# Closing rows in two column groups and two stores with two-dimensional patterns, in a decode layer on one core

## Chip, core, metric

One core of a Trainium2 chip. The metric is the device time of one execution in microseconds (us).

In the profile PE is TensorE, PEld its weight loads, DVE VectorE, ACT ScalarE, POOL GpSimd and SP SyncE; a q marks an engine's sequencer, which issues DMAs. A landing is the semaphore update that tells that data has arrived. The granted clock is the share of TensorE's full clock that its throttle let through.

## The reference

One decode step for 4 sequences: a layer norm modulated by a small matrix product, attention of 32 heads over the last 1024 keys and values of a cache, a second modulated norm and a feed-forward layer of 1792 units. Cut to what the argument needs:

```python
mod = (silu(c) @ w_mod).reshape(4, 6, 1, -1)          # sa, ca, ga, sb, cb, gb
x = x + ga * attention(layernorm(x) * (1 + ca) + sa)  # keys, values: 8 MB each; wq, wo: 4 MB each
h = layernorm(x) * (1 + cb) + sb
x = x + gb * (relu(h @ w1) @ w2)                      # w1 512x1792, w2 1792x512
```

The output is 4 rows of 512 bf16 values, 4 KB; the inputs are 32 MB.

## The kernel before

Everything is loaded once, in one queue issued by SP, in the order of use; w2 comes last, in five pieces of 4, 4, 3, 2 and 1 blocks of 128 rows. The last product has only 4 rows, so its 512 columns are cut into four pieces of 128 which run side by side in the four 32-column groups of TensorE. The rows of one piece lie on partitions 0, 8, 16 and 24 of the group's 32 (`BS = 8`):

```python
BS = CG // B                                  # CG = 32, B = 4
cx_sb = work.tile([2 * B, D], bf16, name="cx_sb")
nc.scalar.dma_start(out=cx_sb[0:B, :], in_=c)
nc.scalar.dma_start(out=cx_sb[B:2 * B, :], in_=A_x.rearrange("b o d -> (b o) d"))
...                                           # loads on nc.sync; constants by GpSimd
W2_CHUNKS = [(0, 4), (4, 4), (8, 3), (11, 2), (13, 1)]
...
def ffn2(m0, m1):
    for m in range(m0, m1):
        for nh in range(NH):                  # NH = 4 column groups
            nc.tensor.matmul(out=z_ps[nh * CG:(nh + 1) * CG, :], lhsT=uT32[:, m, :],
                             rhs=w2_sb[:, m, nh * DH2:(nh + 1) * DH2],
                             start=(m == 0), stop=(m == FT - 1), tile_position=(0, nh * CG))
...
nc.vector.tensor_tensor(out=zg[:], in0=z_ps[:], in1=gb2[:], op=ALU.mult)
nc.vector.tensor_tensor(out=res[:], in0=zg[:], in1=x12_ps[:], op=ALU.add)
nc.scalar.dma_start(out=out.rearrange("b o (g n) -> (o g) b n", g=NH), in_=res[::BS, :])
```

## Time and profile before

| | before |
|---|---|
| time, median of the runs beside the changed kernel | 85.73 us (85.61 to 85.98) |
| span of the profiled run (its time: 85.97 us) | 84.2 us |
| HBM read | 31.99 MB, mean 380 GB/s |
| last landing of w2 in the profiled run | 80.62 us |
| from there to the end (the tail) | 3.57 us |

The span is shorter than the time, which also holds the start and end of an execution. The tail is what can be changed without touching the loads; the prediction shows its lines.

### The profile page before, as it was taken

Reading aid. Unit: us, or ns where it says so; the run is one execution under the profiler, and the core shown is the slowest. Engines: PE = TensorE matmul, PEld = TensorE weight load, DVE = VectorE, ACT = ScalarE, POOL = GpSimd, SP = SyncE. Lnnn points to the kernel's source line nnn. Section 1 sums busy time; section 2 is a strip of 40 time slices with the busy share of each in tenths; the row PEclk is TensorE's granted clock in tenths of the full one; section 3 lists DMA queues with packets and bytes.
Section 4 is the critical chain, followed back from the end, with each engine's and each line's share of the span. In section 5 each row is a group of like instructions: output and inputs, shape, how many; then the busy total and the mean of one; then the engine's idle time right before and its main releaser. Section 6 shows DMA issues by size and latency. Waiting matters only on the chain.

```text
span 84.2 us, 2368 instructions
## 1 busy us (share of the span) xinstructions
PE 56.2 (67%) x1064; PEld 47.2 (56%) x1064; DVE 25.7 (31%) x73; ACT 23.6 (28%) x37; POOL 5.2 (6%) x20
## 2 busy tenths in 40 slices
PE   0001006999972889999999941999727579598730
PEld 0000006996772883997777801999727239588610
DVE  0104000348133100164665476950001320251320
ACT  2301001664302000487788718640100010001000
POOL 6980000000000000000000000000000000000000
PEclk9999999999996555599999999559755555555555
DMA  2799999999989999999999999999999999999500
GB/s 31 301 457 455 386 432 471 459 483 420 389 370 405 424 424 424 401 428 424 409 420 420 420 420 416 416 424 428 409 416 424 416 415 432 418 387 399 186 1 2
DMA packets 4221, 32.14 MB, mean 382 GB/s; under 512 B 492, under 2 KB 628, under 8 KB 1268
## 3 DMA queue, kind: packets, MB, share of 16 engines
q1 hardware_dynamic: 4176, 31.98, 91.7%
q8 instruction: 8, 0.13, 0.6%
q10 hardware_dynamic: 36, 0.01, 0.1%
q14 instruction: 1, 0.01, 0.0%
HBM read 31.99 MB, written 0.00 MB: 380 GB/s over the span
## 4 chain that ended last, share of the span: by engine, by line
DMA 93%; SPq 2%; PE 1%; DVE 1%; issue 0%
DMA v<-in_A_v_cache_dram 33%; DMA wo_sb<-in_A_wo_dram 24%; DMA w<-in_B_w_dram 19%; DMA k<-in_A_k_cache_dram 16%; PE z_ps L472 1%; SPq L81 1%; SPq L91 0%; SPq L90 0%; DVE zg L482 0%; DVE res L484 0%
## 5 line engine op out<-in xcount | busy, mean ns | idle before, releaser
L204 PE MATMUL ktp<-ident_k,k 128*128 128x128 bf16 x256 | 19.1, 247 | 6.5 <-DMA k<-in_A_k_cache_dram 6.5
L204 PEld LDWEIGHTS <-k 128*128 128x128 bf16 x256 | 18.1, 113 | 9.1 <-DMA k<-in_A_k_cache_dram 6.6
L209 ACT COPY kT<-ktp 128x1024 bf16<-128x1024 bf16 x16 | 15.6, 1015 | 19.0 <-PE ktp L204 18.0
L207 DVE COPY kT<-ktp 128x1024 bf16<-128x1024 bf16 x16 | 11.1, 692 | 18.0 <-PE ktp L204 17.7
L342 PE MATMUL oT_ps<-pT,v 128*128 128x16 bf16 x256 | 7.1, 172 | 2.0 <-issue 2.0
L342 PEld LDWEIGHTS <-v 128*128 128x128 bf16 x256 | 7.0, 100 | 2.1 <-issue 2.0
L216 PE MATMUL sc_ps<-kT,qpad 128*32 128x512 bf16 x64 | 5.6, 445 | 0.4 <-DVE qpad L308 0.4
L359 PE MATMUL pT_ps<-ident_bf,p_rep 128*128 128x128 bf16 x32 | 3.2, 282 | 2.9 <-DVE p_rep L353 2.9
L179 PE MATMUL tp<-ident_bf,cx_sb 8*128 8x8 bf16 x4 | 0.3, 169 | 6.6 <-DMA cx_sb<-in_A_x_dram 6.6
L359 PEld LDWEIGHTS <-p_rep 128*128 128x128 bf16 x32 | 2.8, 131 | 3.4 <-DVE p_rep L353 3.4
L304 PE MATMUL qT_ps<-hT,wq_sb 128*128 128x4 bf16 x128 | 3.5, 166 | 1.4 <-DVE ab L297 1.4
L304 PEld LDWEIGHTS <-wq_sb 128*128 128x128 bf16 x128 | 3.5, 104 | 1.5 <-issue 1.5
L179 PEld LDWEIGHTS <-cx_sb 8*128 8x128 bf16 x4 | 0.2, 112 | 6.6 <-issue 6.6
L411 ACT COPY y<-y_ps 128x256 f32<-128x256 f32 x1 | 0.4, 372 | 9.3 <-DVE y L410 9.3
L353 DVE TENSOR_TENSOR p_rep<-e_sb,mi 128x512 int32<-128x512 int32 x4 | 2.5, 687 | 0.7 <-ACT e_sb L348 0.7
L472 PE MATMUL z_ps<-w,uT 128*32 128x128 bf16 x56 | 2.2, 303 | 0.7 <-DMA w<-in_B_w_dram 0.5
L384 DVE TENSOR_TENSOR oT_sb<-oT_ps,rb 128x128 bf16<-128x128 f32 x1 | 0.3, 291 | 7.8 <-PE oT_ps L342 7.8
L418 PEld LDWEIGHTS <-wo_sb 128*128 128x128 bf16 x64 | 2.5, 120 | 0.4 <-DMA wo_sb<-in_A_wo_dram 0.4
L418 PE MATMUL y_ps<-o,wo_sb 128*128 128x4 bf16 x64 | 2.4, 173 | 0.3 <-DMA wo_sb<-in_A_wo_dram 0.3
L414 PEld LDWEIGHTS y_ps<-sel_b,y 128*128 128x128 f32 x8 | 1.8, 327 | 1.4 <-DVE y L410 1.4
L406 PE MATMUL y_ps<-wo_sb,o 128*32 128x512 bf16 x16 | 1.9, 628 | 0.9 <-DVE o L397 0.9
L216 PEld LDWEIGHTS <-qpad 128*32 128x32 bf16 x64 | 1.3, 103 | 2.2 <-DVE qpad L308 0.7
(107 smaller groups left out, 51.9 us busy)
## 6 DMA issues: line engine op xcount, KB each, us to landing
k<-in_A_k_cache_dram SPq DMA_DIRECT2D x8, 1024.0 KB, 28.1
v<-in_A_v_cache_dram SPq DMA_DIRECT2D x8, 1024.0 KB, 20.1
wq_sb<-in_A_wq_dram SPq DMA_DIRECT2D x1, 4096.0 KB, 22.5
wo_sb<-in_A_wo_dram SPq DMA_DIRECT2D x4, 1024.0 KB, 20.4
wmod_sb<-in_w_mod_dram SPq DMA_DIRECT2D x1, 2304.0 KB, 9.7
w<-in_B_w_dram SPq DMA_DIRECT2D x1, 1792.0 KB, 21.9
w<-in_B_w_dram SPq DMA_DIRECT2D x2, 512.0 KB, 19.5
wmod_sb<-in_w_mod_dram SPq DMA_DIRECT2D x1, 768.0 KB, 4.6
```

The costliest lines, as they stand in the source:

```text
L204: nc.tensor.transpose(out=tp[:, ii, :], in_=k_tiles[gi][:, iq * IQ + ii, :], identity=ident_k)
L207: nc.vector.tensor_copy(out=dst, in_=tp[:])
L209: nc.scalar.copy(out=dst, in_=tp[:])
L216: nc.tensor.matmul(out=sc_ps[hw * CG:(hw + 1) * CG, half * HALF:(half + 1) * HALF], lhsT=qpad[:, b, par, hw, :], rhs=kT[:, half * (NI // 2 ...
L304: nc.tensor.matmul(out=qT_v[:, hq, :], lhsT=wq_sb[:, t, hq * Dh:(hq + 1) * Dh], rhs=hT[:, t, :], start=(t == 0 and hq == 0), stop=(t == DT ...
L342: nc.tensor.matmul(out=oT_ps[:, hw, par].rearrange("p b r -> p (b r)"), lhsT=v_tiles[h][:, i, :], rhs=pT[:, i, c0:c0 + B * rep], start=(fi ...
L353: nc.vector.tensor_tensor(out=p_w[:, ws, :], in0=e_w[:, ws].unsqueeze(2).to_broadcast([P, WQ // 2, B]), in1=mi4[:].unsqueeze(1).to_broadca ...
L359: nc.tensor.transpose(out=tp[:, ii, :], in_=p_rep[:, i // 2, :, i % 2], identity=ident_bf[:])
L406: nc.tensor.matmul(out=y4_ps[q0:q0 + CG, :], lhsT=o4[:, l, g % 2, g // 2, :], rhs=wo_sb[:, g, l, :], start=(g == 0 and l < 4), stop=(g == ...
L414: nc.tensor.matmul(out=y_ps[:, t, :], lhsT=y4[:, t, :], rhs=sel_b[:], start=(t == 0), stop=False)
L418: nc.tensor.matmul(out=y_ps[:, m, :], lhsT=wo_sb[:, g, l, m::DT], rhs=o4[:, l, g % 2, g // 2, 0:B], start=False, stop=(g == NP - 1 and l = ...
L472: nc.tensor.matmul(out=z_ps[nh * CG:(nh + 1) * CG, :], lhsT=uT32[:, m, :], rhs=w2_sb[:, m, nh * DH2:(nh + 1) * DH2], start=(m == 0), stop= ...
```

## The change

The intent is a cheaper store. Two column groups carry the 512 columns, each in two turns: turn 0 leaves its rows on even partitions, turn 1 adds its rows on odd ones, because the weights of turn 1 are the same columns read one element earlier. So each group ends with 8 consecutive rows, stored with a two-dimensional pattern, one group by SP, the other by ACT. The two groups left free take blocks 0 to 3 of w2, which are added in ahead of time. x moves to GpSimd's queue. Cut to its core:

```diff
-    BS = CG // B
+    NX = 2
+    CP = CG + NX
-    nc.scalar.dma_start(out=cx_sb[B:2 * B, :], in_=A_x.rearrange("b o d -> (b o) d"))
+    nc.gpsimd.dma_start(out=cx_sb[B:2 * B, :], in_=A_x.rearrange("b o d -> (b o) d"))
 ...
+    def put(tile3):
+        return tile3[:, :, NX:NX + NX * B:NX]
+    def rows(tile3, j, x):
+        return tile3[:, j, NX - x:NX - x + CG]
+    def closing(parts):
+        for x in range(NX):
+            for (ps, q, j, src, rhs, start, stop, cols) in parts:
+                for g in range(2):
+                    q0 = (q + g) * CG
+                    nc.tensor.matmul(out=ps[q0:q0 + CG, cols], lhsT=rows(src, j, x), rhs=rhs(2 * x + g),
+                                     start=start and x == 0, stop=stop and x == NX - 1, tile_position=(0, q0))
 ...    # gb and x12 go through closing() too; siluT32, uT32 and xs2 are CP = 34 columns wide
+    for m in range(ZA):                       # ZA = 4: blocks 0-3 in groups 2 and 3
+        closing([zpart(m), zpart(ZA + m)])
+    nc.scalar.copy(out=zc[:], in_=za_ps[2 * CG:P, :])
+    nc.vector.tensor_tensor(out=zc[:], in0=zc[:], in1=gb2[:], op=ALU.mult)
+    nc.vector.tensor_tensor(out=zc[:], in0=zc[:], in1=x12_ps[:], op=ALU.add)
+    for m in range(2 * ZA, FT):
+        closing([zpart(m)])
 ...
-    nc.vector.tensor_tensor(out=res[:], in0=zg[:], in1=x12_ps[:], op=ALU.add)
-    nc.scalar.dma_start(out=out.rearrange("b o (g n) -> (o g) b n", g=NH), in_=res[::BS, :])
+    nc.vector.tensor_tensor(out=res[:], in0=zg[:], in1=zc[:], op=ALU.add)
+    out_v = out.rearrange("b o (x g n) -> (b o x) g n", x=NX, g=2)
+    nc.sync.dma_start(out=out_v[:, 0, :], in_=res[0:NX * B, :])
+    nc.scalar.dma_start(out=out_v[:, 1, :], in_=res[CG:CG + NX * B, :])
```

## The prediction

> **What bounds the kernel now.** I read the page's DMA row first, then the chain that ended last, then the last microseconds in the timeline, then single rows for the instructions that the change touches.
>
> The chain in order of time:
> ```profile
> 0.73 0.37 SPq L90
> ...
> 15.81 28.16 DMA v<-in_A_v_cache_dram
> ...
> 43.99 20.36 DMA wo_sb<-in_A_wo_dram
> ...
> 64.37 15.92 DMA w<-in_B_w_dram
> 80.28 0.04 issue
> 80.33 0.66 PE z_ps L472 x11
> 80.99 0.02 issue
> 81.01 0.30 DVE zg L482
> 81.31 0.02 issue
> 81.34 0.29 DVE res L484
> ```
> Nearly the whole chain is one stream of loads. The page's DMA row shows 9 tenths in nearly every slice up to the end of that stream, so the loads are never short of requests. 31.99 MB at 380 GB/s are 84.2 us: no load is removed, so about 80.3 of the 84.2 us cannot be touched by this change. What it can touch is the tail, from the landing of the last pieces of w2 to the end.
>
> The tail in the timeline (start, duration, engine, line, operation):
> ```profile
> 78.25 1.10 PE L472 MATMUL z_ps<-w,uT 128*32 128x128 bf16 x32 [0.21 <-DVE uT L467]
> ...
> 79.66 0.51 PE L472 MATMUL z_ps<-w,uT 128*32 128x128 bf16 x12 [0.31 <-DMA w<-in_B_w_dram]
> ...
> 80.33 0.64 PE L472 MATMUL z_ps<-w,uT 128*32 128x128 bf16 x12 [0.15 <-DMA w<-in_B_w_dram]
> ...
> 81.01 0.29 DVE L482 TENSOR_TENSOR zg<-z_ps,gb 128x128 f32<-128x128 f32 x1 [2.28 <-PE z_ps L472]
> 81.34 0.29 DVE L484 TENSOR_TENSOR res<-zg,x_ps 128x128 bf16<-128x128 f32 x1
> 81.66 0.60 ACTq L485 DMA_DIRECT2D out_dram<-res  x1
> ```
> The reader is to see that the closing matmuls run in bursts, each released by a landing, and that nothing lies beside the last steps. The store is issued at 81.66. In the single records its first packet moves at 82.91, 1.25 us after the issue began; the packets take 0.11 us; the last of its four landings comes at 83.36. From there to 84.19 there are only the closing semaphores and barriers, 0.8 us that the change leaves alone.
>
> Rows of DMA issues (duration min/median/max in ns), which show what a pattern of more dimensions costs its sequencer:
> ```profile
> L485 ACTq DMA_DIRECT2D out_dram<-res x1: 602/602/602, 81.7 to 81.7; - x1
> ```
> ```profile
> L103 SPq DMA_DIRECT2D v<-in_A_v_cache_dram x8: 535/535/535, 15.8 to 41.6; - x8
> ```
> ```profile
> L127 SPq DMA_DIRECT2D w<-in_B_w_dram x5: 327/328/328, 56.7 to 66.8; - x5
> ```
> ```profile
> L71 ACTq DMA_DIRECT2D cx_sb<-in_c_dram x1: 568/568/568, 0.7 to 0.7; - x1
> ```
> ```profile
> L72 ACTq DMA_DIRECT2D cx_sb<-in_A_x_dram x1: 265/265/265, 1.3 to 1.3; - x1
> ```
> The k, v loads and the store have three-dimensional patterns: 535 and 602 ns. The w2 loads have two: 328. Four rows on ACT took 265, but 568 when SP was issuing at the same moment.
>
> **What the Trainium skill says.** Perfetto Trace Analysis, section "DMA Instruction — HWDGE", says that a DMA issue's span in the profile runs over the wait for a lock, the use of a descriptor generator that two sequencers share, and the push of excess semaphore counts. The 568 ns beside the 265 agree with a shared generator; one case does not prove it. DMA: Bandwidth & Descriptors, "Why a DMA increments its semaphore by 16 and not by 1", says that the number of engines is the largest up to 16 that divides the slowest dimension of both sides, and that the issuing sequencer adds the rest of 16. The old store (4x4x128 against 16 rows) should use 4: the trace has one early update and four landings, which agrees. The new stores, 8x128 each, should use 8. TensorE: Matmul & The Clock Gate, "Back-to-back issue gap", gives N / 1.2 ns between matmuls at the cold clock, 107 ns for N = 128. The records of the closing matmuls start in fours, a few ns apart within a four and 106 ns from four to four, with a granted clock of 0.50 from 76 us on: it agrees.
>
> **The change, part by part.**
>
> *x by GpSimd's queue.* ACT loses one issue of 0.27 us, GpSimd gains one before its first memset. x is needed by the first transposes, which now wait until 6.6 us; TensorE then has nothing until the first k tile at 13.36. So x may land up to 6 us later at no cost. GpSimd's set-up ends at 6.0 us and its first product with a close user, the identity for the k transposes, stands at 1.84 against 13.36. A microsecond or several more there is hidden. The order of SP's loads is the same in the changed kernel, and from the sixth k load on each waits for the same earlier load. Effect: 0.
>
> *gb and x12 in two column groups.* The matmul count is unchanged, 16 each, but gb now has two per column group and t. Its 4 fours of 106 ns become 8 pairs of 106: about +0.4 us of TensorE near 21 us. That delays the modulation, q and scores by 0.4. Loads have about 20 us between issue and landing, so the stream does not notice; and later TensorE waits for wo and again 0.43 us for w1, which absorbs it. x12 ends at 75.74 and w1 lands at 76.12. Effect: 0.
>
> *The closing matmuls.* Blocks 0 to 7 run as four pairs, still four column groups at once: 8 fours, as before. But block 4 now stands beside block 0, so the pair waits for the second w2 chunk, whose last landing is 78.69. From 78.73, 8 fours of 106 ns end before 79.62, where the third chunk lands: hidden. Blocks 8 to 13 have only two groups. Blocks 8 to 10: 6 pairs, 79.66 to 80.30, just in time for the fourth chunk (80.28). Blocks 11 and 12: 4 pairs. The first ends at 80.59 (as the first four does now), then 80.70, 80.80, 80.91. Block 13's chunk lands at 80.62, but TensorE is still streaming; its two pairs end at 81.02 and 81.12. Now they end at 80.96. Effect: **+0.16 us** on the path.
>
> *The added work.* One ACT copy (0.25, as the copy of gb) and two DVE operations (0.29 each) on the upper half: from about 79.9 to 80.8, before zg starts at about 81.17. Hidden. zg and res keep 128 columns; half the partitions save nothing[...]. res reads SBUF instead of PSUM: the scaling of the identity from SBUF, also 128 columns, took 285 ns against 287, so 0. No wait is lengthened by them.
>
> *The stores.* Two issues, one each on SP and ACT, of 8 rows with two dimensions. From issue start to first packet the three-dimensional store took 1.25 us; c's load on ACT, two-dimensional and beside SP's issue, took 0.95 (0.74 to 1.69). So **-0.30 us**, even with the other sequencer in the way. One data descriptor per engine instead of four: the packets take perhaps 0.03 instead of 0.11, **-0.07**. The wait for the write's landing, 0.34, stays.
>
> Sum: +0.16 - 0.30 - 0.07 = -0.21 us. 85.74 - 0.2 = about **85.55 us**.
>
> **The rivals.** First, *the two issues block each other*: both wait for the same DVE operation and start within nanoseconds. If one generator serves them in turn and the second takes 0.57 or more, as c did, plus a cold start on ACT after 80 us without an issue, the store path gains only the 0.07 and the matmuls cost 0.16: 85.85. For it speaks 568 against 265; against it that c's first packet came soon all the same and that its partner had 128 rows, not 8.
>
> Second, *TensorE becomes the bound of the tail*. Counted from the second chunk's landing at 78.69, the changed kernel has 20 steps of 106 ns, 2.1 us, ending within a few hundredths of the load-bound count. Odd weight offsets (the second column set starts one 2-byte element off) or late fours could cost 10 to 30 ns a step; with 12 steps after the third chunk that would be +0.1 to +0.35, so 85.65 to 85.9. Against it: weight loads of 32 columns lie under the running matmul in the present trace.
>
> Third, *the issue gain is all there and nothing else is lost*: if SP and ACT do not meet and each issue takes 0.27 to 0.33 us, the landing may come 0.4 earlier, and with the other terms as above 85.4. Fourth, *the software queue costs something outside the chain*, a delayed start of the stream or a longer end on GpSimd: nothing in the trace of before can show it, since no load uses that queue; I allow +0.3.
>
> **Range and chances.** The three parts on the path are a few tenths each, with opposite signs. The rivals span 85.4 to 85.9, and the three runs of before spread over 0.16, with the profiled run at 85.97; other chips add as much. So 85.1 to 86.0 for 8 in 10. Two per cent is 1.7 us; to gain that, more than half of the 3.6 us after the last landing would have to vanish, and to lose it, a new wait of 1.7 us would have to appear. Chances: faster 0.01, within 2% 0.975, slower 0.015.
>
> **What would show each step right or wrong.** In the changed profile: the stream of w still ends at about 80.3 to 80.6; the last closing matmul ends about 0.5 us after the last landing instead of 0.34; zg and res at 0.29 each; two issues of 0.27 to 0.35 (a pair of one short and one near 0.57 would speak for the first rival); first store packet about 0.95 us after res; the end about 0.2 us earlier than 84.2. The copy and the two DVE operations on the upper half must end before the last matmul. TensorE's wait for x should be below 13 us; the DMA row should stay at 9 tenths. The prediction is wrong if the first weight load or the k transposes wait for GpSimd, if zg waits for the upper half, or if the stores land later after res than the present 1.73 us.

## The result, and the profile after

85.62 us (85.49 to 85.68, 6 runs) against 85.73 (85.61 to 85.98). Ratios here are the mean time of one kernel's runs over that of the other's of the same rounds, so not quite the ratio of the medians quoted: 0.9982, 95% interval 0.9966 to 0.9999, that is 0.15 us less. That is the same by the mark of 2%, and a gain that the interval only just tells from none; the time lies inside the predicted range.

The tail of the changed kernel in the timeline:

```profile
79.48 0.26 ACT L497 COPY zc<-za_ps 64x128 f32<-64x128 f32 x1 [3.56 <-PE za_ps L194]
79.78 0.28 DVE L498 TENSOR_TENSOR zc<-zc,gb 64x128 f32<-64x128 f32 x1 [1.32 <-ACT zc L497]
80.10 0.28 DVE L499 TENSOR_TENSOR zc<-zc,x_ps 64x128 f32<-64x128 f32 x1
80.93 0.28 DVE L504 TENSOR_TENSOR zg<-z_ps,gb 64x128 f32<-64x128 f32 x1 [0.55 <-PE z_ps L194]
81.25 0.28 DVE L506 TENSOR_TENSOR res<-zg,zc 64x128 bf16<-64x128 f32 x1
81.56 0.37 SPq L508 DMA_DIRECT2D out_dram<-res  x1
81.56 0.31 ACTq L509 DMA_DIRECT2D out_dram<-res  x1
```

The added copy and its two operations end at 80.38, and zg still waits 0.55 us for TensorE (the bracket): they are hidden. The stores are issued in 0.37 and 0.31 us instead of 0.60, though at the same moment.

Because two profiled runs end their streams at different moments whatever the kernel, the tails are best laid side by side from the last landing of w2. From the single records of both traces, in us:

| step | before | after | difference | predicted |
|---|---|---|---|---|
| last landing of w2 to end of the last matmul | 0.342 | 0.544 | +0.202 | +0.16 |
| from there to the result | 0.660 | 0.637 | -0.023 | 0 |
| result to last landing of the output | 1.732 | 1.419 | -0.313 | -0.37 |
| from there to the end of the span | 0.834 | 0.908 | +0.074 | 0 |
| sum (rounded) | 3.568 | 3.508 | -0.06 | -0.21 |

The third row is itself a sum: 0.03 from the result to the issue, from the start of the issue to the first packet 1.249 before and 0.787 after (-0.46), from the first packet's start to the last one's 0.10 and 0.09, and from there to the last landing 0.35 and 0.51 (+0.16). (The prediction counted to the end of the last packet, hence its 0.11 and 0.34.)

The chain that ended last looks quite different in this profile (page, part 4):

```profile
DMA 61%; PE 30%; DVE 3%; issue 1%; SPq 1%; ACT 1%; DVEq 0%
```

It was 93% DMA. The reader should not take this for a new bound. The chain followed another branch at a v load, which waited for TensorE to free a k buffer, at most 0.5 us (SP's own waits):

```profile
SPq L105 <- PE ktp L225: 1.2, 3, 0.5
```

That load was put behind some 20 us of queued loads, and the DMA row stays at 9 tenths.

### The profile page after: what moved, and what is told of

Its sections match the earlier page's. It is cut to its first block, busy times and chain, and to the rows that moved or that the text cites. A ratio compares the mean times of both kernels' runs of the same rounds, so it can differ in the third digit from the quotient of the medians.

```text
span 83.9 us, 2373 instructions
## 1 busy us (share of the span) xinstructions
PE 56.3 (67%) x1064; PEld 47.6 (57%) x1064; DVE 26.3 (31%) x76; ACT 23.9 (28%) x38; POOL 5.9 (7%) x21
## 4 chain that ended last, share of the span: by engine, by line
DMA 61%; PE 30%; DVE 3%; issue 1%; SPq 1%; ACT 1%; DVEq 0%
DMA v<-in_A_v_cache_dram 24%; DMA w<-in_B_w_dram 23%; PE ktp L225 14%; DMA k<-in_A_k_cache_dram 14%; PE qT_ps L322 4%; PE sc_ps L237 3%; PE z_ps L194 3%; PE mT L273 2%; PE mT L275 1%; PE m_ps L259 1%; PE m_ps L262 1%; PE st_ps_var L289 1%; PE gb_ps L194 1%; SPq L93 0%; SPq L92 0%
## 5 line engine op out<-in xcount | busy, mean ns | idle before, releaser
L194 PEld LDWEIGHTS <-uT 128*32 128x32 bf16 x56 | 2.2, 136 | 0.8 <-DMA w<-in_B_w_dram 0.4
```

What stands on the lines that cost most here:

```text
L194: nc.tensor.matmul(out=ps[q0:q0 + CG, cols], lhsT=rows(src, j, x), rhs=rhs(2 * x + g), start=start and x == 0, stop=stop and x == NX - 1, ...
```

## The experiments

My theory at this point: the closing matmuls cost 0.20 us because each step takes 106 ns, the store pattern saves 0.3 us, the rest is neutral. Rivals: x's queue is what helped; two sequencers are what helped; landings set the tail and the groups don't matter.

### x alone, and all but x

`e1_x_on_act` puts x back on ACT in the changed kernel; `e2_x_alone` moves x and nothing else in the kernel before.

```diff
-    nc.gpsimd.dma_start(out=cx_sb[B:2 * B, :], in_=A_x.rearrange("b o d -> (b o) d"))
+    nc.scalar.dma_start(out=cx_sb[B:2 * B, :], in_=A_x.rearrange("b o d -> (b o) d"))
```

> The changed kernel with x put back on ACT's queue. My theory (x's queue is off the path): the load stream ends where it does in the changed kernel within the scatter of runs (last landing of w2 at 80.3 to 80.7 us), the tail from that landing to the end stays 3.5 us but for the closing barriers, which shrink from 0.91 to about 0.83 us because GpSimd's part of them is shorter without a software queue; time equal to or up to 0.1 us below the changed kernel's, ratio to before 0.996 to 0.999. Rival (moving x is what starts or ends the stream earlier and is the larger part of the 0.15 us gained): the stream ends about 0.2 us later than in the changed kernel and the ratio goes back to 1.000.

> The kernel before with x on GpSimd's queue and nothing else. My theory: closing barriers 0.08 us longer, nothing else; ratio 1.000 to 1.002. Rival (x's queue brings the gain): the last landing of w2 comes about 0.2 us earlier and the ratio is 0.997 to 0.998.

Measured: ratios 0.9976 (0.9956 to 0.9997) and 1.001 (0.999 to 1.003); the last landings of w2 at 80.33 and 80.37 us. The gain stays without the move and doesn't come with it: the rival falls. (In the changed kernel x landed at 7.25 us instead of 6.48 and the first transposes started at 7.29 instead of 6.62, well ahead of 13.2, where k is first used.)

The end of the span is less simple than I expected. GpSimd's last drain, semaphore clearing and drain take 0.078 + 0.096 + 0.034 us in the kernels without a load on its queue (5 other such kernels: at most 0.004 more) and 0.102 + 0.139 + 0.040 with one (7 other such kernels: 0.275 to 0.281 in sum): 0.07 us, as the changed kernel's last row shows. Yet e1's end was not shorter but longer, 0.997 us. Its trace shows why: SP checks the load semaphores in a fixed order, some 60 ns for each check, and without x on the other queue the stores take another pair of the eight: one store's semaphore stood fourth from the last check, so three checks were still to be made after its landing. For the same reason e2's end, 0.961, was 0.13 longer than before and not the 0.08 expected: one more check came after its store's. The move of x thus costs 0.07 us at one place of the end and spares 0.16 at another. Both are below what the timed runs resolve.

### The store's pattern

`e3_four_2d` cuts the one store of the kernel before into four two-dimensional ones, still from partitions 8 apart:

```diff
+    out_v = out.rearrange("b o (g n) -> (b o) g n", g=NH)
+    for g in range(NH):
+        eng = nc.sync if g % 2 == 0 else nc.scalar
+        eng.dma_start(out=out_v[:, g, :], in_=res[g * CG:(g + 1) * CG:BS, :])
```

> The kernel before (closing rows in four column groups) with its one store of three dimensions split into four stores of two dimensions, 4 rows each, two on SP and two on ACT. My theory (the number of dimensions sets the issue and the delay to the first packet): each issue takes 0.27 to 0.37 us, the first packet moves about 0.8 us after the first issue begins as in the changed kernel, the second pair about 0.35 us later, so the last landing comes about 1.65 to 1.75 us after the result is ready, against 1.73 before and 1.42 in the changed kernel; ratio 0.998 to 1.001. Rival A (splitting over two sequencers is what helps, whatever the dimensions): the landing comes by 1.5 us or sooner, and with the matmul tail of before the time beats the changed kernel, ratio 0.996. Rival B (landings of stores on the same engines queue behind each other, about 0.18 us each): the four groups of landings are 0.15 to 0.2 us apart.

Measured: 87.29 us, ratio 1.0171 (1.0146 to 1.0196). My theory and rival A were both missed: each issue is slow although the pattern has two dimensions, and there are two in a row on each sequencer.

```profile
L488 SPq DMA_DIRECT2D out_dram<-res x2: 638/692/747, 81.4 to 82.2; - x2
L488 ACTq DMA_DIRECT2D out_dram<-res x2: 602/651/700, 81.4 to 82.1; - x2
```

The last landing came 2.80 us after the result. Rival B fits the first two stores only, whose packets moved together and whose landings are 0.18 apart; the next two, 0.46 and 0.37 later, follow their own later packets. So I formed another theory: the step between the partitions, not the number of dimensions, makes it slow. Three runs tell them apart. `e9_stride2` is the changed kernel with its rows on every second partition (`CP` and `ident_m` follow):

```diff
-        return tile3[:, :, NX:NX + NX * B:NX]
+        return tile3[:, :, 2 * NX:2 * NX + 2 * NX * B:2 * NX]
-        return tile3[:, j, NX - x:NX - x + CG]
+        return tile3[:, j, 2 * (NX - x):2 * (NX - x) + CG]
-    nc.sync.dma_start(out=out_v[:, 0, :], in_=res[0:NX * B, :])
+    nc.sync.dma_start(out=out_v[:, 0, :], in_=res[0:2 * NX * B:2, :])      # ACT's likewise
```

> The changed kernel with the closing rows on every second partition of their column group instead of on consecutive ones; both stores still have 8 rows and two dimensions, the result is right. Theory formed after the four-store run (it is the step between partitions in SBUF, not the number of dimensions, that makes the issue and the first packet slow): issues of 0.6 to 0.75 us, first packet 1.25 to 1.35 us after the issue begins instead of 0.79, the end 0.5 us later, ratio 1.003 to 1.006. Rival (dimensions or the number of rows decide, as the prediction had it): issues of 0.30 to 0.37 us, first packet at 0.8, ratio 0.998.

```profile
L508 SPq DMA_DIRECT2D out_dram<-res x1: 793/793/793, 81.9 to 81.9; - x1
L509 ACTq DMA_DIRECT2D out_dram<-res x1: 721/721/721, 81.9 to 81.9; - x1
```

First packet 1.37 us after the issue begins: a step between partitions is enough to make a two-dimensional store slow. The ratio was 1.0105 (1.0083 to 1.0126), more than expected; its loads were slower as well, of which below. `e11_3d_unit_wrong` takes the three-dimensional pattern of before, from consecutive partitions. Its output is wrong, which doesn't matter for the time.

```diff
-    nc.sync.dma_start(out=out_v[:, 0, :], in_=res[0:NX * B, :])
-    nc.scalar.dma_start(out=out_v[:, 1, :], in_=res[CG:CG + NX * B, :])
+    nc.scalar.dma_start(out=out.rearrange("b o (g n) -> (o g) b n", g=NH), in_=res[0:NH * B, :])
```

> The changed kernel with one store on ACT in exactly the three-dimensional pattern of the kernel before (4x4x128 to HBM, 16 source rows), but from 16 consecutive partitions; the rows do not hold the whole result, so it is wrong on purpose. Step theory: issue 0.30 to 0.40 us, first packet about 0.8 us after it begins. Dimension theory (the prediction's): issue 0.55 to 0.6 us, first packet at 1.2 to 1.25. The time of the first is 0.2 to 0.3 below that of the second; ratio 0.998 against 1.001.

```profile
L508 ACTq DMA_DIRECT2D out_dram<-res x1: 702/702/702, 81.6 to 81.6; - x1
```

First packet at 1.35 us, ratio 1.004 (1.002 to 1.006): three dimensions are enough as well. So neither theory alone is right: a short issue needs both, two dimensions and consecutive partitions. The two costs don't add (before had both, 602 ns). What e11 leaves open is whether the third dimension costs, or the four rows to each landing that come with it: its 16 rows have four landings, those of `e4_one_2d_wrong` below sixteen. Four landings alone don't make a store slow, as `e10_four_unit` shows. Why this issue takes 702 ns where that of before takes 602 stays open.

`e10_four_unit` gives the kernel before consecutive rows, 4 in each group, and four stores:

```diff
-    nc.vector.tensor_scalar_max(out=uT32[:, m0:m1, ::BS], in0=us[:], scalar1=0.0)
+    nc.vector.tensor_scalar_max(out=uT32[:, m0:m1, 0:B], in0=us[:], scalar1=0.0)   # siluT32, xs2 likewise
-    nc.scalar.dma_start(out=out.rearrange("b o (g n) -> (o g) b n", g=NH), in_=res[::BS, :])
+    for g in range(NH):                                        # out_v = (b o) g n
+        eng = nc.sync if g % 2 == 0 else nc.scalar
+        eng.dma_start(out=out_v[:, g, :], in_=res[g * CG:g * CG + B, :])
```

> The kernel before with its four result rows of each column group on consecutive partitions (0 to 3 of 32) and four stores of 4 rows, two on SP and two on ACT; the result is right. Step theory: issues of 0.27 to 0.37 us, first packet about 0.8 us after the first issue begins, the second pair 0.3 to 0.4 later, last landing 1.5 to 1.75 us after the result; with the last matmul 0.34 us after the last landing of w2 the tail is within 0.15 of the changed kernel's; ratio 0.996 to 1.000. Rival (a store of 4 rows on 4 engines is slow whatever its step, as the four-store run would also allow): issues of 0.6 to 0.75 and a ratio of 1.015 or more, as in that run.

```profile
L490 SPq DMA_DIRECT2D out_dram<-res x2: 273/310/348, 80.8 to 81.2; - x2
L490 ACTq DMA_DIRECT2D out_dram<-res x2: 279/294/308, 80.8 to 81.1; - x2
```

Four rows are as quick as eight. But the landings of the four stores, four each, end at 81.95, 82.13, 82.31 and 82.49 us, 0.18 apart, although their packets moved in two close pairs. (The trace doesn't tell which engines carried them.) The same 0.18 parts the two stores of the changed kernel (82.76 and 82.95): this is the +0.16 of its third row. The ratio was 0.992 (0.9903 to 0.9937), below all expectation, and not by its tail: at 3.90 us it missed the expected 0.15 around the changed kernel's, with the landing 1.75 after the result and five more checks of SP after the store's own (an end of 1.14). Its last landing of w2 came at 79.74.

`e4_one_2d_wrong` prices a single store, 16 consecutive rows. Its output is wrong, which doesn't matter for the time.

```diff
-    nc.sync.dma_start(out=out_v[:, 0, :], in_=res[0:NX * B, :])
-    nc.scalar.dma_start(out=out_v[:, 1, :], in_=res[CG:CG + NX * B, :])
+    nc.scalar.dma_start(out=out.rearrange("b o (g n) -> (b o g) n", g=NH), in_=res[0:2 * NX * B, :])
```

> The changed kernel with one store of 16 rows and two dimensions on ACT in place of the two of 8 rows; it stores rows that do not hold the result for the second half, so it is wrong on purpose: it is the price of a single store. Theory that the second store's landing waits for the first's (in the changed kernel ACT's eight landings end at 82.76 and SP's at 82.95 though their packets move at the same time): one store lands 1.2 to 1.25 us after the result is ready instead of 1.42, and the ratio is 0.996. Rival (the late landing is a matter of the addresses or of SP's own longer issue): the landing stays at 1.35 to 1.45 us and the ratio at 0.998.

```profile
L508 ACTq DMA_DIRECT2D out_dram<-res x1: 339/339/339, 81.8 to 81.8; - x1
```

The last landing came 1.38 us after the result instead of 1.42; ratio 0.9991 (0.9965 to 1.0018). So the expected 1.2 to 1.25 was missed, and the number is the rival's. The parts say why: there is no second landing to wait for, and the landing comes 0.38 after the packets instead of 0.51, but with 16 rows the first packet comes at 0.83 instead of 0.79 and the packets take 0.14 instead of 0.09. A single store would not have been worth more closing steps. And as one sequencer does as well as two, two sequencers are not what helped.

### The closing matmuls

`e6_no_upper` runs all 14 blocks in the two lower groups:

```diff
-    for m in range(ZA):
-        closing([zpart(m), zpart(ZA + m)])
-    nc.scalar.copy(out=zc[:], in_=za_ps[2 * CG:P, :])          # and the two operations on zc
-    for m in range(2 * ZA, FT):
+    for m in range(FT):
         closing([zpart(m)])                                    # zpart: always z_ps, groups 0 and 1
```

> The changed kernel with all 14 blocks of w2 in the two lower column groups, so without the upper pair of groups, the copy and the two operations on it. Step theory (the closing matmuls are a count of steps of 106 ns at the halved clock): 28 steps follow the first without a wait that matters, so the last matmul ends about 27 x 0.106 + 0.31 = 3.2 us after the first begins, and 0.75 to 0.85 us after the last landing of w2 instead of 0.54; the tail is 0.2 to 0.3 us longer than the changed kernel's, ratio 1.000 to 1.002. Rival (landings set the tail, the groups do not matter): the distance stays at 0.55 us and the ratio at 0.998.

The last matmul ended 0.59 us after the last landing, not 0.75 to 0.85, and 2.93 us after the first began, not 3.2. The single records give the reason: 23 of the 27 steps between start times are 106 or 107 ns, the first is 79, and the last three are 64, 56 and 55. The windows show what happened then (columns: stretch, its length, busy time of the five engines, granted clock, DMA share, GB/s):

```profile
79.00:80.00 1.00, 1.00 (x24) 1.00 (x22) 0.00 (x0) 0.00 (x0) 0.00 (x0) 0.50 0.29 107
80.40:80.90 0.50, 0.47 (x14) 0.30 (x10) 0.00 (x0) 0.00 (x0) 0.00 (x0) 0.92 0.00 0
```

At 80.48, after 2.5 us of matmuls without a pause, the granted clock rose from 0.50 to 1.00, and the rest ran at nearly twice the pace. So the count of steps was right and the clock I multiplied by was not constant. Without the rise the end would have come about 0.24 us later (an estimate: the last three steps 42 to 51 ns shorter, the last matmul 0.22 instead of 0.31 us), at the expected 0.83. The rise seems to belong to the profiled run alone: it took 85.62 us at a mean clock of 0.796, the other five 85.72 to 86.03 at 0.756 to 0.777. What raised the clock no run isolates. The ratio, 1.0003 (0.9983 to 1.0023), lies at the lower end of what the step theory expected; its interval overlaps the changed kernel's 0.9966 to 0.9999, so the worth of the upper groups isn't settled beyond "small".

`e7_warm` adds matmuls nobody reads, to keep the clock up:

```diff
+    def warm(n):
+        for _ in range(n):
+            nc.tensor.matmul(out=sc_ps[:, 0:512], lhsT=ident_bf[:], rhs=pT[:, 0:4, :], start=True, stop=True)
+    ...                       # calls of 9, 3, 5, 3, 3, 3, 4, 4 and 1 in the gaps from value tile v6 on
```

> The changed kernel with some 30 matmuls of 512 columns added, whose result nobody reads, in the gaps where TensorE waits from 60 us on, to keep its clock from being halved. Theory (the closing matmuls cost the tail 0.20 us because each step takes 106 ns at the halved clock): if the granted clock is 0.9 or more from 78 us on, the steps come 55 to 65 ns apart and the last matmul ends 0.30 to 0.37 us after the last landing of w2 instead of 0.54; ratio to before 0.995 to 0.997. If the clock stays at 0.5, nothing changes but for delays of up to 0.2 us. Rival (the 0.20 us is weight loading at an odd offset or the issue of matmuls): with the clock raised the distance stays near 0.5 us.

86.64 us, ratio 1.0111 (1.0078 to 1.0144), against 0.995 to 0.997 expected: I had placed too many. (The profiled run is the slowest of the six, 87.39 us.) The nine of the first call started late and ran at half clock:

```profile
63.25 3.62 PE L396 MATMUL sc_ps<-pT,ident_bf 128*128 128x512 bf16 x8 [0.23 <-issue]
```

All later work was pushed past the loads: the last matmul ended 2.09 us after the last landing in that run. The clock did stay at 1.00 from 70 us on, and the closing steps then came 55 to 56 ns apart, so the size of a step is the clock's doing and not that of the odd weight offset. But whether a warm clock shortens the tail was not tested, since nothing in that tail waited for a landing.

### Where the loads land in SBUF

e10's stream was the puzzle. One thing differs in it that was not meant to: a new constant, `ident_m`, makes the constants ahead of the load buffers 64 bytes a partition larger, which puts every load buffer at a multiple of 512 bytes. In the kernel before they stand at 448 modulo 512, in the changed kernel at 128, in e9 at 224 (addresses as the build of each kernel assigns them). `e12_before_aligned` adds nothing but 64 unused bytes to the kernel before:

```diff
+    pad = const.tile([P, 16], f32, name="pad")     # e13: [P, 32] in the changed kernel
+    nc.gpsimd.memset(pad[:], 0.0)
```

> The kernel before with 64 bytes a partition of unused memory ahead of the load buffers, so that every load's destination starts at a multiple of 512 bytes instead of 448 modulo 512. Address theory (the four-unit run's stream ended 0.6 to 0.9 us early because its buffers happened to stand at multiples of 512): 4 MB take 9.5 us instead of 9.6 in the middle of the stream, the last landing of w2 comes at 79.6 to 79.9 us instead of 80.3 to 80.6, ratio 0.991 to 0.994. Rival (something else in that kernel, such as its stores or its contiguous rows, made the stream faster): ratio 0.998 to 1.002.

> The changed kernel with 128 bytes a partition of unused memory, so that the loads' destinations stand at 256 modulo 512 instead of 128. If a multiple of 256 is enough: the stream ends at 79.6 to 79.9 us and the ratio is 0.989 to 0.992. If it takes a multiple of 512: as the changed kernel, 0.997 to 0.999.

84.83 us, ratio 0.9876 (0.9856 to 0.9896), and for e13 84.70 us, ratio 0.9868 (0.9848 to 0.9887). Both are more than the theory expected. Last landings of w2 at 79.22 and 79.33; tails 3.57 and 3.51, as without the padding. The windows of 40 to 70 us, where only v, wo and w1 are loaded, show it best (last column GB/s): before, after, e12 and e13 in turn.

```profile
40.00:70.00 30.00, 23.24 (x496) 18.96 (x493) 12.60 (x23) 11.82 (x20) 0.00 (x0) 0.77 1.01 418
```
```profile
40.00:70.00 30.00, 23.25 (x490) 18.98 (x488) 12.18 (x23) 11.40 (x20) 0.00 (x0) 0.76 1.01 419
```
```profile
40.00:70.00 30.00, 23.59 (x502) 19.20 (x499) 12.00 (x23) 11.22 (x19) 0.00 (x0) 0.76 1.01 424
```
```profile
40.00:70.00 30.00, 23.64 (x502) 19.28 (x500) 12.04 (x23) 11.24 (x19) 0.00 (x0) 0.76 1.01 425
```

e9 has 417, e10 425. Over all runs, starts at 0 modulo 256 give 424 to 425 GB/s (four kernels), starts at 128, 192 and 224 give 417 to 420 (ten). The single records show it packet by packet: in this window a packet of 8 KB took on average 310.6 to 310.7 ns in the kernels at 0, 314.4 to 315.0 at 128, 315.5 at 192 and 316.5 at 224. (That is 4 to 6 ns a packet; the 14 KB packets of w1 save about as much, 539 against 542 to 544 ns, those of 18 and 32 KB nothing that stands out.) A multiple of 256 is enough. The Trainium skill (DMA: Bandwidth & Descriptors, "How a descriptor splits into AXI transactions") says that reads of less than a full transaction must start at a 256-byte boundary and that a descriptor starting elsewhere fetches unused bytes; here it is the destination that was moved, and the measured cost is 1.1 to 1.2% of the time (0.9876 against 1, and 0.9868 against 0.9982). This padding, of no part of the change, brings six to seven times what the change brings. e13 has the lowest median of the correct kernels; e12's interval overlaps its own.

`e14_best` was meant to add two more small things to it (its padding is 384 bytes, for a multiple of 512):

```diff
-    nc.gpsimd.dma_start(out=cx_sb[B:2 * B, :], ...)
+    nc.scalar.dma_start(out=cx_sb[B:2 * B, :], ...)
-    W2_CHUNKS = [(0, 4), (4, 4), (8, 3), (11, 2), (13, 1)]
+    W2_CHUNKS = [(0, 8), (8, 3), (11, 2), (13, 1)]
```

> The version that the runs point to: the changed kernel with load buffers at multiples of 512 bytes, x back on ACT's queue (no software queue, closing barriers 0.07 us shorter) and the first two pieces of w2 as one load, which makes the two stores take the last two of the eight load semaphores, checked last at the end. Expected: stream end 79.6 to 79.9 us, last matmul 0.55 us and result 1.18 us after it, last landing 1.42 after the result, end 0.83 after that: ratio 0.989 to 0.991. If the address theory falls: ratio 0.996 to 0.998.

85.02 us, ratio 0.9916 (0.9895 to 0.9936): slower than e13. The end did shrink to 0.834 us, but the last matmul ended 0.91 us after the last landing. The layout of w2 sets the order of w1's columns, so with a piece of 8 blocks the first layer reads the weights of blocks 0 to 7 with a step of 8 elements instead of 4 (weight loads of that layer in the changed kernel, then in e14: count, then busy us and mean ns):

```profile
L479 PEld LDWEIGHTS <-w 128*128 128x128 bf16 x56 | 1.8, 112 | 0.8 <-DMA w<-in_B_w_dram 0.8
```
```profile
L481 PEld LDWEIGHTS <-w 128*128 128x128 bf16 x56 | 2.7, 141 | 0.8 <-DMA w<-in_B_w_dram 0.8
```

These means mix all 14 blocks. In the single records the 32 loads of blocks 0 to 7 took 168 ns each and started 60 ns apart, against 118 and 33 in the changed kernel, and the means of the other 24 differ by 2 ns or less. That is 0.9 us more on TensorE just before the closing matmuls.

## Why the prediction was right

- **The stream is the bound and isn't touched.** Right as to the bound, and the reason why nothing of the change could matter much; that the buffers' addresses moved with the constants was overlooked (see the total). The last landing came at 80.35 us after and 80.62 before; e2 and e3, whose loads are those of the kernel before, ended at 80.37 and 80.35, so the 0.27 us between the two profiles is scatter of runs in the main (the profiled run of before was a long one, 85.97 us).
- **x and gb, no effect.** Right: the k transposes began at 13.22 us instead of 13.36 and x12 ended at 75.23, before w1 landed at 75.88. One named sign of being wrong came close: the page puts the wait of the first transposes, at 7.29, down to GpSimd's last memset, which ended at 7.26, just as x landed. It cost nothing.
- **Closing matmuls, +0.16.** Measured +0.20, the mechanism as told. The steps are 106 to 108 ns, blocks 11 and 12 still run when block 13 lands (80.35; its first matmul starts at 80.45). About 0.03 of the rest is that the two matmuls of a pair start 27 ns apart where those of a four started a few ns apart.
- **Added work hidden.** Right, with 0.55 us to spare.
- **Stores, -0.30 and -0.07.** The sum, -0.37, was near the measured -0.31, but out of wrong terms. The first packet came 0.46 earlier, not 0.30, as the two issues hardly delayed each other (the first rival: 0.37 and 0.31 us side by side, where one with 128 rows had stretched 265 ns to 568). The packets gained 0.01, not 0.07. And "the wait for the write's landing, 0.34, stays" was wrong: the two stores, with the eight landings each that it expected, land 0.18 apart, and it grew by 0.16. That these errors nearly cancelled is luck. The cause named, dimensions, is one of two: a step between partitions costs as much (e9, e11).
- **The end "that the change leaves alone".** Wrong by 0.07: the fourth rival allowed +0.3 for the software queue, and this is its part at the end.
- **The total.** -0.21 predicted, -0.15 measured by time (interval -0.29 to -0.01), -0.06 by the two tails. The tenth between the last two isn't settled, but the record points at the loads: the change also moved the buffers from 192 to 128 modulo 256, and by the packet times above (315.5 against 314.4 to 315.0 ns) that is worth 0.1 to 0.2 us over some 60 us of such loads (an estimate; no run isolates it, and scatter of the stream's end is as large). Where both kernels start at multiples of 256, e12 and e13, the change is worth 0.0008 of the ratio, 0.07 us, with intervals that overlap, and 0.05 by the tails. So what was predicted, cheaper stores against dearer matmuls, brought a quarter to a third of the 0.21, and that the total came nearer is, by this estimate, luck.
- **The range.** A slip: 1.7 us is a little less than half of 3.6 us, not more. It changes nothing.

## What to carry to other kernels

When a kernel is one long stream of loads, look at what the loads cost per byte before polishing its end: a start of every load buffer at a multiple of 256 bytes was worth 1.2% here, and any change that adds or removes a small constant can shift it unseen, so two kernels are compared at equal starts. For the last store, put the rows on consecutive partitions and keep the pattern at two dimensions; two stores were better than four, as their landings came one after the other. Compare tails from the last landing on, term by term, since a total that agrees may be made of terms that do not.

## What the Trainium skill lacked or had wrong

- DMA: Bandwidth & Descriptors: no price of a store by its pattern. Here 0.27 to 0.37 us of issue and 0.77 to 0.83 to the first packet with two dimensions and consecutive partitions; 0.60 to 0.79 and 1.25 to 1.37 with a third dimension or a partition step.
- The same page, "How a descriptor splits into AXI transactions": speaks of reads. A destination in SBUF off a multiple of 256 bytes costs too: 417 to 420 against 424 to 425 GB/s.
- The same page, "Queues, rings and completion order", HWDGE ordering: says that a semaphore write lands after earlier writes of its engine, without a number. Two stores whose packets moved together landed 0.18 us apart.
- TensorE: Matmul & The Clock Gate, "LDWEIGHTS (loading the stationary operand)": gives the time by the number of columns alone. With a step of 8 elements between columns a load took 168 ns and the next started 60 ns later, against 118 and 33 with a step of 4. No page that I read has a time by this step.
- No page that I read: GpSimd's part of a kernel's end is 0.07 us longer if its queue was used, and SP's checks of the load semaphores at the end are some 60 ns each, so a store should use those checked last.
